# Zero fills moved from GpSimd to the vector engine, the last output projection cut into five full banks, and a new order of the whole program

## The chip, the core and the metric

The kernel runs on one NeuronCore of a Trainium2 chip. Its engines are named here as the profile names them: PE (TensorE, matmuls into PSUM), PEld (its weight loads), DVE (VectorE), ACT (ScalarE), POOL (GpSimd) and SP (SyncE, which in this kernel issues nearly all DMAs). The metric is device microseconds (us) of one execution.

## The reference

Two independent layers over 2048 tokens and 640 features (bf16), whose results stand side by side in one output of 1280 columns.

```python
# A: gated long convolution, columns 0..639
k_shift = sum(k_pad[:, t:t+S] * shift_k[:, 3-t] for t in range(4))
kv = k_shift * v
y = irfft(rfft(kv, 2S) * rfft(ssm_k, 2S))[:S] + kv * ssm_D
a = q * y
# B: segmented attention with a memory, columns 640..1279; 32 heads of 20, N=4 segments of 512
for s in range(4):
    p = softmax(qs @ ks.T * scale + mask)      # mask: -1e9 on keys after the query
    a_dot = p @ vs
    a_mem = (phi(qs) @ M) / (phi(qs) @ z + 1e-6)
    outs.append(g * a_mem + (1 - g) * a_dot)
    M, z = M + phi(ks).T @ vs, z + phi(ks).sum()
b = concat(outs) @ wo
```

## The kernel before

Layer A runs in five blocks of 128 channels (`conv(dp)`). For each block the short filter is a set of matmuls with `kr` (the keys, transposed by the DMA) as weights ("ks"), multiplied by `vt` on DVE. The Fourier transforms are matmuls with the table `Wf`: of the long filter `kT` and of `vt` ("F" groups, eight banks of 512 columns each). DVE does butterflies and the product (`Kh`, `Xh`, `Y`, `pq`), and the inverse is matmuls with `Wi`.

Layer B runs in eight units `u` (`project(u)`, `attend(u)`): segment `u // 2`, half `u % 2` of the heads. `project` makes K, Q and V of four token tiles (five matmuls of 320 columns each, tile `KQ` for K and Q, `Va` for V), turns K and Q into `KQT` (in unit 0 by matmuls with the identity, later by a DMA), and writes a bound of the logits into spare rows of `KQT` by four small DMAs from `bT`. `attend` makes logits in PSUM (weights from `KQT`), exponentials on ACT (`ET`, two of 128x1024 for every set of four heads), and the weighted values by matmuls with `ET` as weights; DVE divides and adds them into `o_s`. `project_out(s)` turns `o_s` and multiplies by `wo`. In the last segment (`last`) the turn is done by matmuls with the identity, one bank for each of five column chunks `cc` of `o_s`, and each bank goes to `xT`.

A row of attention pads and constants is filled once at the start: the unused columns of `KQ`, `PP` (the feature maps phi), `kmx`, the first columns of `kr` and `kb`, and the two memories `Mbd`. `PP[:, 0]` is phi of K and is not written in the last segment; `PP[:, 1]` is phi of Q.

No instruction is issued where it is written: `Recorder.add` (line 151) records every operation, and `issue` (line 245) emits them all from line 257 in the order of a table of numbers (`ORDER`, line 890). `BASE` (line 911) gives each PSUM group its bank, and `EVICT` (line 885) says for each copy out of PSUM whether DVE ("1") or ACT ("0") does it. Each engine then works through its own part of that order, one instruction after the other, and waits at an instruction until what it needs is there. So a late load holds up all that stands behind it on the engine that waits. SP issues DMAs in order too, and the ninth DMA and each later one first waits until the one eight places before it, on the same semaphore, has landed.

The copy that `EVICT` decides is

```python
def evict(self, out, in_, grp):
    ...
    if EVICT[e] == "1":
        self.nc.vector.tensor_copy(out=out, in_=in_, grp=grp)
    else:
        self.nc.scalar.copy(out=out, in_=in_, grp=grp)
```

At the start `WARM` matmuls on a zeroed tile (`o2`, ten of 512 columns) run on PE before there is data.

Of the kernel before, what the change touches and what calls it, by code (L numbers as in the profile page):

```python
# [21 lines left out]
S = 2048; D = 640  # L22
H = 32; DH = 20; NS = 4; L = 512
# [3 lines left out]
KPAD = 16  # L27
# [238 lines left out]
class Layer:  # L266
    def __init__(self, ctx, tc, A_q, A_k, A_v, A_shift_k, A_ssm_k, A_ssm_D, B_x, B_wq, B_wk, B_wv, B_wo, B_beta, out):
# [5 lines left out]
        E = ctx.enter_context  # L273
# [90 lines left out]
        nc.gpsimd.memset(self.PP[:, 1, :, :, DH + 1:DH + 2], 1.0)  # L364
        nc.gpsimd.memset(self.kr[:, 0:KPAD], 0.0)
        self.kb = c.tile([128, KPAD + S], bf16, name="kb")
        nc.gpsimd.memset(self.kb[:, 0:KPAD], 0.0)
# [4 lines left out]
        for h in range(2):  # L372
            nc.gpsimd.memset(self.Mbd[h][0][:], 0.0)
# [459 lines left out]
    def project_out(self, s):  # L833
        nc, rec = self.nc, self.rec
        last = s == NS - 1
        if last:
# [11 lines left out]
            spare = self.PP[:, 0].rearrange("p t h d -> p (t h d)")  # L848
        else:
            oTv = self.ring("xT", None)[:].rearrange("p c q -> p (c q)").rearrange("p (t c q) -> p t c q", t=4, c=5)  # L850
            for t in range(0, 4, 2):
                rec.key = ("oT", s, t)
                nc.sync.dma_start_transpose(out=oTv[:, t:t + 2].rearrange("p t c q -> p (t c) q"), in_=self.o_s[s][:, t:t + 2])
        for t in range(4):
            rec.key = ("W", s, t)
            if last and t < 3:
                outb = spare[:, 640 * t:640 * t + 640].rearrange("p (i j) -> p i j", i=2)
            else:
                outb = self.ring("outb", [128, 2, 320], n=2)[:]
            for i in range(2):  # L860
                if i % WW == 0:
                    g = self.group(WW, "w")
                for part in ((0, 1, 2), (3,), (4,)) if last else ((0, 1, 2, 3, 4),):
                    with rec.one():
                        for cc in part:
                            nc.tensor.matmul(g.ap[:, i % WW, 0:320], lhsT=oTv[:, t, cc, :], rhs=self.wo[:, cc, 320 * i:320 * i + 320], start=(cc == 0), stop=(cc == 4), grp=g)
# [18 lines left out]
EVICT = ("1110001010000101101001001000000000000000000000000000000000010000000000000000000001000100000000100000000000000000000000000000001000000000"  # L885
         "000000000000000100000000001001000000001000100010011000110100000010011010000001101100000010000000000000")
# [100 lines left out]
```

## Time and profile before

| | us |
|---|---|
| median of three runs (lowest, highest) | 273.2 (272.6, 273.31) |
| the profiled execution | 274.12 |
| its span, first to last instruction | 272.3 |
| PE busy | 261.3 (96%) |
| DVE busy | 250.4 (92%) |
| ACT busy | 247.3 (91%) |
| POOL busy | 6.8 (3%) |

The profiled execution is 1.82 us longer than its span, and 0.92 us above the median of the three runs. "Busy" of PE includes matmuls that stand in its pipeline, so 96% doesn't mean PE at its peak. Nearly all instructions have line 257, so they are told apart by tiles: `ET<-ps` is an exponential, `KQ<-ps` a copy of a projection, `F<-ps` one of a transform, and so on. An "x4" in a row of the timeline means four such instructions merged, and the duration then reaches from the first one's start to the last one's end. A bracket says how long the engine had been idle and what ended it.

### The profile page before, as it was taken

The numbers are of one execution on the slowest core, as the hardware profiler recorded it, in microseconds if no ns is written. First come the engines' busy times: TensorE is split into PE (matmuls) and PEld (weight loads), VectorE is DVE, ScalarE is ACT, GpSimd is POOL, SyncE is SP. The second block draws the span as 40 slices with busy tenths as digits, with TensorE's granted clock in tenths as the row PEclk, the third lists the DMA queues.
The fourth block names the chain that finished last, engine by engine and source line by source line (L and its number), as shares of the span: only waits on it lengthen the run. The fifth ranks groups of instructions, "written<-read, shape, count | busy, mean of one in ns | idle before, by whom it ended". The sixth has DMA issues, their size and how long they took to land.

```text
span 272.3 us, 10125 instructions
## 1 busy us (share of the span) xinstructions
PE 261.3 (96%) x4385; PEld 196.4 (72%) x4387; DVE 250.4 (92%) x395; ACT 247.3 (91%) x377; POOL 6.8 (3%) x18
## 2 busy tenths in 40 slices
PE   8789999999999999999999999999999999998994
PEld 3568767868867677776766787768576876766883
DVE  1799999999999999999999999999999999999950
ACT  2356899999999999999999999999999999899954
POOL 8100000000000000000000000000000000000000
PEclk9799999999999999999999999999999999899999
DMA  6999399999959678996896989959964566454233
GB/s 163 293 242 214 70 223 207 211 291 137 182 102 231 214 156 145 177 186 128 167 204 161 224 178 150 178 117 186 197 140 123 59 139 108 85 67 116 75 70 105
DMA packets 126716, 43.73 MB, mean 161 GB/s; under 512 B 117083, under 2 KB 124256, under 8 KB 126544
## 3 DMA queue, kind: packets, MB, share of 16 engines
q1 hardware_dynamic: 126512, 42.91, 79.7%
q8 instruction: 34, 0.56, 0.8%
q0 software_dynamic: 160, 0.19, 0.2%
q14 instruction: 10, 0.08, 0.1%
HBM read 14.11 MB, written 7.34 MB: 79 GB/s over the span
## 4 chain that ended last, share of the span: by engine, by line
PE 60%; ACT 24%; DVE 10%; issue 4%; ACTq 0%; DVEq 0%
PE ps L257 60%; ACT ET L257 15%; ACT F L257 4%; DVE Kh L257 2%; ACT Va L257 2%; DVE F L257 1%; DVE o L257 1%; ACT outb L257 1%; ACT KQ L257 1%; ACT PP L257 1%; DVE pq L257 1%; DVE vt L257 1%; DVE Xh L257 1%; ACT bT L257 1%; DVE qabs L257 0%
## 5 line engine op out<-in xcount | busy, mean ns | idle before, releaser
L257 ACT ACTIVATE ET<-ps 128x1024 bf16<-128x1024 f32 x160 | 165.2, 1140 | 1.0 <-PE ps L257 0.9
L257 PEld LDWEIGHTS <-xT 128*128 128x128 bf16 x640 | 59.0, 98 | 27.2 <-issue 6.4
L257 PE MATMUL ps<-wqkv,xT 128*128 128x320 bf16 x480 | 75.4, 299 | 1.2 <-ACT ET L257 0.6
L257 ACT CAST F<-ps 128x512 bf16<-128x512 f32 x71 | 44.6, 721 | 1.9 <-PE ps L257 1.7
L257 PE MATMUL ps<-Va,ET 128*128 128x21 bf16 x1280 | 41.7, 173 | 0.1
L257 PEld LDWEIGHTS <-ET 128*128 128x128 bf16 x1280 | 39.3, 96 | 2.5 <-issue 1.4
L257 PEld LDWEIGHTS <-Wf 128*128 128x128 bf16 x320 | 29.6, 99 | 7.5 <-DMA Wf<-c_wf 1.3
L257 PE MATMUL ps<-KQT 32*128 32x128 bf16 (+2 forms) x896 | 34.0, 240 | 0.4 <-ACT ET L257 0.3
L257 ACT CAST KQ<-ps 128x320 bf16<-128x320 f32 x52 | 25.3, 537 | 4.2 <-PE ps L257 4.1
L257 PE MATMUL ps<-wo,xT 128*128 128x320 bf16 x160 | 26.4, 304 | 0.6 <-ACT ET L257 0.5
L257 PE MATMUL ps<-kT,Wf 128*128 128x256 bf16 x160 | 23.5, 283 | 1.5 <-DVE kT L257 1.3
L257 PEld LDWEIGHTS <-KQT 32*128 32x128 bf16 x896 | 16.1, 92 | 10.3 <-issue 8.7
L257 PE MATMUL ps<-vt,Wf 128*128 128x256 bf16 x160 | 22.1, 273 | 0.0
L257 PE MATMUL ps<-Y,Wi 128*128 128x256 bf16 x160 | 20.5, 273 | 0.0
L257 PE MATMUL ps<-Mbd,PqT 128*128 128x84 bf16 x96 | 18.2, 203 | 1.0 <-ACT ET L257 0.8
L257 DVE TENSOR_TENSOR Y<-Y,pq 128x2048 bf16<-128x2048 bf16 (+1 forms) x20 | 18.8, 952 | 0.1
L257 DVE TENSOR_TENSOR pq<-Xh,Kh 128x2048 bf16<-128x2048 bf16 x15 | 18.1, 1209 | 0.0
L257 PEld LDWEIGHTS <-Wi 128*128 128x128 bf16 x160 | 14.6, 98 | 3.6 <-issue 1.5
L257 ACT ACTIVATE PP<-KQ 128x1280 bf16<-128x1280 bf16 x12 | 16.7, 1389 | 0.0
L257 PEld LDWEIGHTS <-kr 128*128 128x128 bf16 x116 | 14.7, 149 | 2.2 <-issue 0.4
L257 ACT CAST Va<-ps 128x320 bf16<-128x320 f32 x28 | 14.5, 547 | 0.3 <-PE ps L257 0.2
L257 PE MATMUL ps<-pack 32*128 32x128 bf16 x512 | 14.4, 218 | 0.3 <-ACT ET L257 0.2
(90 smaller groups left out, 373.4 us busy)
## 6 DMA issues: line engine op xcount, KB each, us to landing
vt<-in_A_v_dram SPq DMA_DIRECT2D x10, 256.0 KB
pq<-in_A_q_dram SPq DMA_DIRECT2D x10, 256.0 KB
out_dram<-outb SPq DMA_DIRECT2D x13, 160.0 KB
turned<-kT SPq DMA_DIRECT2D x4, 512.0 KB
kT<-turned SPq DMA_DIRECT2D x4, 512.0 KB
out_dram<-pq SPq DMA_DIRECT2D x8, 256.0 KB
kb<-kr SPq DMA_DIRECT2D x6, 256.0 KB
Wf<-c_wf SPq DMA_DIRECT2D x4, 256.0 KB
```

The source lines that it names most:

```text
L257: f(*[fix(a) for a in args], **{k: fix(v) for k, v in kw.items()})
```

## The change

Three edits.

1. Nine fills of constants (line 360 to 373) go from POOL to DVE; `Drow` stays on POOL. Those of zeros over 2-byte elements are issued over 4-byte elements on DVE, so that their counts are halved (`KQ` 128x1536 becomes 128x768).
2. In the last segment the output projection no longer makes eight groups of 320 columns (four token tiles, two halves). The four tiles of 640 columns are laid side by side, 2560 columns, and cut into five banks of 512. A bank that covers two token tiles takes two matmuls per chunk `cc`, one for each tile's piece, of 128, 256 or 384 columns. All five results go to `PP` (in place of three to `PP[:, 0]` and the fourth to `outb`), and four stores go out from there.
3. `ORDER`, `BASE` and `EVICT` are replaced, and `EVICT` has 235 digits with 32 ones in place of 238 with 36.

```diff
-        nc.gpsimd.memset(self.kmx[:, :, DH:32], 0.0)
-        nc.gpsimd.memset(self.KQ[:, :, :, :, DH:32], 0.0)
-        nc.gpsimd.memset(self.KQ[:, :, 0, :, DH:DH + 1], 1.0)
-        nc.gpsimd.memset(self.PP[:, :, :, :, DH:32], 0.0)
+        nc.vector.memset(self.kmx[:, :, DH:32], 0.0)
+        nc.vector.memset(self.KQ[:, :, :, :, DH:32], 0.0)
+        nc.vector.memset(self.KQ[:, :, 0, :, DH:DH + 1], 1.0)
+        nc.vector.memset(self.PP[:, :, :, :, DH:32], 0.0)
...
         for h in range(2):
-            nc.gpsimd.memset(self.Mbd[h][0][:], 0.0)
+            nc.vector.memset(self.Mbd[h][0][:], 0.0)
...
-            spare = self.PP[:, 0].rearrange("p t h d -> p (t h d)")
...
+        if last:
+            flat = self.PP[:].rearrange("p a t h d -> p (a t h d)")[:, 0:2560]
+            for b in range(5):
+                rec.key = ("W", s, b)
+                g = self.group(1, "w")
+                pieces = [(t, max(0, 512 * b - 640 * t), min(640, 512 * b + 512 - 640 * t)) for t in range(4)]
+                pieces = [p for p in pieces if p[1] < p[2]]
+                for part in ((0, 1, 2), (3,), (4,)):
+                    with rec.one():
+                        for t, lo, hi in pieces:
+                            for cc in part:
+                                nc.tensor.matmul(g.ap[:, 0, 640 * t + lo - 512 * b:640 * t + hi - 512 * b], lhsT=oTv[:, t, cc, :], rhs=self.wo[:, cc, lo:hi],
+                                                 start=(cc == 0 and t == pieces[0][0]), stop=(cc == 4), grp=g, skip_group_check=True)
+                self.evict(flat[:, 512 * b:512 * b + 512], g.ap[:, 0, :], g)
+            for t in range(4):
+                rec.key = ("OB", s, t)
+                self.stores(last).dma_start(out=self.out[L * s + 128 * t:L * s + 128 * t + 128, D:2 * D], in_=flat[:, 640 * t:640 * t + 640])
+            return
         for t in range(4):
...
-            if last and t < 3:
-                outb = spare[:, 640 * t:640 * t + 640].rearrange("p (i j) -> p i j", i=2)
-            else:
-                outb = self.ring("outb", [128, 2, 320], n=2)[:]
+            outb = self.ring("outb", [128, 2, 320], n=2)[:]
...
-EVICT = ("1110001010000101101001001000000000000000000000000000000000010000...
+EVICT = ("0101000110000010100000101000000000000000000000000000000000000000...
```

What the new tables do is seen from the order of the instructions on each engine, before and after. Three places matter below.

First SP at the start, which issues the loads: `Y` receives the first tokens `x`, `kT` the long filter, `kr` the transposed keys, `wqkv` the weights of the projections, `vt` the values of layer A. Before:

```order
L257 DMA ident<-c_ident 128x128
L257 DMA kT_99<-in_A_ssm_k_dram 128x2048
L257 DMA Y_98<-in_B_x_dram 128x640
L257 DMA Wf<-c_wf 128x1024
L257 DMA Y_98<-in_B_x_dram 128x640
L257 DMA Wf<-c_wf 128x1024 x3
L257 DMA Y_98<-in_B_x_dram 128x640 x2
L257 DMA wqkv<-in_B_wk_dram 128x5x320
L257 DMA_TRANSPOSE kr<-in_A_k_dram 128x2048
L257 DMA wqkv<-in_B_wq_dram 128x5x320
L257 DMA vt_103<-in_A_v_dram 128x8x128 x2
```

and with the change:

```order
L257 DMA Y_98<-in_B_x_dram 128x640 x2
L257 DMA ident<-c_ident 128x128
L257 DMA Y_98<-in_B_x_dram 128x640
L257 DMA wqkv<-in_B_wk_dram 128x5x320
L257 DMA Y_98<-in_B_x_dram 128x640
L257 DMA_TRANSPOSE kr<-in_A_k_dram 128x2048
L257 DMA Wf<-c_wf 128x1024
L257 DMA kT_99<-in_A_ssm_k_dram 128x2048
L257 DMA Wf<-c_wf 128x1024
L257 DMA vt_103<-in_A_v_dram 128x8x128
L257 DMA Wf<-c_wf 128x1024 x2
L257 DMA wqkv<-in_B_wq_dram 128x5x320
```

The tokens, the K weights and the transposed keys come first now, the long filter and its Fourier table behind them: PE begins with the K projection, its turns and the short filter, and does the filter's transform after these.

Second DVE at the start (`o_95` is the tile of the warming matmuls, and later of the sigmoid of beta). Before:

```order
L257 MEMSET o_95 128x320
L257 TENSOR_SCALAR o_95<-o_95 128x64
L257 CAST Va_86<-o_95 128x64x2
L257 CAST kT_100<-ps 128x4x128 x2
L257 CAST Va_85<-o_95 128x64x2
L257 CAST taps<-ps 128x40
L257 TENSOR_TENSOR skd_74<-ident,taps 128x512
L257 CAST xT_96<-ps 128x5x128
```

and with the change:

```order
L257 MEMSET PP 128x128x6
L257 MEMSET o_95 128x320
L257 MEMSET kr 128x8
L257 CAST xT_96<-ps 128x5x128
L257 MEMSET KQ 128x128x6
L257 MEMSET Mbd_93 128x176
L257 CAST xT_96<-ps 128x5x128
L257 MEMSET KQ 128x4x16
L257 MEMSET kb 128x8
L257 TENSOR_TENSOR pq_79<-ident,taps 128x512
L257 TENSOR_TENSOR skd_74<-ident,taps 128x512
L257 CAST KQ<-ps 128x16x20 x2
```

The fill of `PP` stands ahead of that of the warming tile, and the sigmoid's TENSOR_SCALAR stands later, behind the copies of K.

Third ACT at the end. Before:

```order
L257 ACTIVATE ET_113<-ps 128x1024
L257 ACTIVATE ET_117<-ps 128x1024 x2
L257 ACTIVATE ET_112<-ps 128x1024 x2
L257 CAST xT_97<-ps 128x512 x2
L257 CAST PP<-ps 128x320 x4
L257 CAST outb_120<-ps 128x320 x2
L257 CAST PP<-ps 128x320 x2
```

and with the change:

```order
L257 ACTIVATE ET_113<-ps 128x1024 x2
L257 ACTIVATE ET_117<-ps 128x1024 x2
L257 ACTIVATE ET_112<-ps 128x1024 x2
L257 CAST xT_97<-ps 128x512 x2
L257 CAST PP<-ps 128x512 x5
```

Eight copies of 320 columns have become five of 512. The copies that ACT does, counted in the two orders, from its first instruction to its first exponential, from there to its last exponential, and behind it:

| copy on ACT | to the first exponential: before, now | between | behind the last |
|---|---|---|---|
| `KQ`, 320 wide | 11, 9 | 41, 46 | 0, 0 |
| `Va`, 320 wide | 3, 2 | 25, 27 | 0, 0 |
| `outb`, 320 wide | 0, 0 | 20, 19 | 2, 0 |
| `F`, 512 wide | 10, 12 | 61, 59 | 0, 0 |
| `KQT`, 512 wide | 8, 7 | 0, 0 | 0, 0 |
| `bT`, 512 wide | 1, 1 | 5, 7 | 0, 0 |
| `xT`, 512 wide | 0, 0 | 3, 2 | 2, 2 |
| `PP`, 320 wide, now 512 | 0, 0 | 0, 0 | 6, 5 |

On DVE there are three `KQ` and one `Va` fewer, one `outb` more; two `bT` fewer, one `KQT` and one `xT` more; and `taps` goes to ACT. PE has 4387 matmuls before and after. Ahead of the first matmul of logits stand 268 of them before and 258 now; the difference is ten matmuls of the projections (75 and 65), and all other kinds have the same count there. POOL issues its four loads in the order `pack`, `skd` (the taps of the short filter), `bt`, `Drow` instead of `bt`, `skd`, `Drow`, `pack`.

More of the change, by code (lines that the diff above doesn't have):

```diff
@@ L862, in project_out @@
                     g = self.group(WW, "w")
[L863 to L866, printed above, removed]
+                with rec.one():
+                    for cc in range(5):
+                        nc.tensor.matmul(g.ap[:, i % WW, 0:320], lhsT=oTv[:, t, cc, :], rhs=self.wo[:, cc, 320 * i:320 * i + 320], start=(cc == 0), stop=(cc == 4), grp=g)
                 if i % WW == WW - 1:
```

54 lines of the change are left out of this document (27 added, 27 removed).

## The prediction

> **What bounds the kernel now.** I read the busy times by stage first, then the chain of waits, then the timelines of the start and the end. I cut the span where ACT starts its first exponential and where it ends its last one.
>
> ```profile
> core 0: us, PE busy (x) PEld busy (x) DVE busy (x) ACT busy (x) POOL busy (x), PEclk, DMA share, GB/s
> 0.00:36.80 36.80, 33.14 (x276) 24.06 (x278) 27.42 (x46) 20.62 (x41) 6.83 (x18) 0.95 0.80 197
> 36.80:261.25 224.45, 220.58 (x4011) 166.65 (x4011) 220.44 (x344) 222.79 (x327) 0.00 (x0) 0.99 0.83 158
> 261.25:272.30 11.05, 7.54 (x102) 5.69 (x98) 2.49 (x6) 3.90 (x10) 0.00 (x0) 0.98 0.34 96
> ```
>
> In the middle ACT is busy 222.79 of 224.45 us, so it is idle for 1.66 us. DVE is idle for 4.01 and PE for 3.87. Three engines are full there at once, and a new order can win next to nothing in it; ACT has the least room. The idle time lies in the first 36.80 us (ACT 16.18, DVE 9.38, PE 3.66) and in the last 11.05 (ACT 7.15). The chain says the same in another way: it runs over all three.
>
> ```profile
> PE 60%; ACT 24%; DVE 10%; issue 4%; ACTq 0%; DVEq 0%
> ```
>
> So I write the span as: start of the first exponential, plus ACT's work from there, plus its 1.66 us of gaps, plus what follows the last exponential. Here are these points, the prices of copies on ACT, and the last store, from the timeline.
>
> ```profile
> 36.80 1.02 ACT L257 ACTIVATE ET<-ps 128x1024 bf16<-128x1024 f32 x1
> 38.94 0.78 ACT L257 CAST KQ<-ps 128x320 bf16<-128x320 f32 x2
> 256.42 4.83 ACT L257 ACTIVATE ET<-ps 128x1024 bf16<-128x1024 f32 x5
> 264.57 1.07 ACT L257 CAST xT<-ps 128x512 bf16<-128x512 f32 x2 [3.32 <-PE ps L257]
> 266.30 1.41 ACT L257 CAST PP<-ps 128x320 bf16<-128x320 f32 x4 [0.65 <-PE ps L257]
> 268.52 0.77 ACT L257 CAST PP<-ps 128x320 bf16<-128x320 f32 x2
> 269.31 0.33 SPq L257 DMA_DIRECT2D out_dram<-PP  x1
> ```
>
> Two copies of 320 columns take 0.78 and four take 1.41, so one more costs (1.41 - 0.78) / 2 = 0.32. Two of 512 take 1.07, 0.53 each.
>
> **ACT's work in the middle.** The two orders' counts: `KQ` +5, `Va` +2, `outb` -1, six more copies of 320 at 0.32: +1.9. `F` -2, `bT` +2, `xT` -1, one fewer of 512 at 0.53: -0.5. Together **+1.4**. Nothing covers it if ACT stays the fullest engine; if ACT had slack, it would cost 0. I take +1.4. DVE gets the reverse: three fewer copies of 320 at 0.483 are -1.4 (one `KQT` and one `xT` more against two `bT` fewer cancel).
>
> ```profile
> L257 DVE CAST KQ<-ps 128x320 bf16<-128x320 f32 x12 | 5.8, 483 | 0.0
> ```
>
> **The fills.** On POOL they cost the span something only through others. On DVE I price them by the one fill that it has already.
>
> ```profile
> 0.88 0.33 DVE L257 MEMSET o<- 128x320 uint32 x1 [0.88 <-PEq L971]
> 5.17 1.40 POOL L257 MEMSET PP<- 128x1536 bf16 x1
> 6.15 1.61 DVE L257 TENSOR_SCALAR o<-o 128x64 f32<-128x64 f32 x1 [4.95 <-ACT o L257]
> 7.80 0.35 DVE L257 CAST Va<-o 128x128 bf16<-128x128 f32 x1
> ```
>
> 320 elements take 0.33, so `KQ` and `PP` with 768 take 0.8 each, the two `Mbd` about 0.2 each, and the five small ones no more than 0.2 each: at most 3.0 in all, and 1 if the size hardly mattered. I take 3.0 and count it as nothing, because DVE has 9.38 us of idle time in that stage; without this cover it is +3.0. `PP`'s fill does delay the warming matmuls by 0.8, but eight of them (at 4.42 / 10 each, row below) then end at 5.6, where ten ended at 5.68.
>
> The TENSOR_SCALAR on 64 elements took 1.61 while POOL was filling; a copy of 128 took 0.35. So up to 1.3 us of the start came from POOL's fills, and it stood ahead of DVE's copies of `kT`, for which PE waited (1.25 us in the row at 9.39 below). The Trainium skill, SBUF — State Buffer, "Who interferes with whom", says that a DVE operation in a 2-port mode and a GpSimd one exclude each other for a whole instruction; the 1.61 agrees. By that rule the 1.3 us go with the fills; by rows alone it stays possible that something else held the TENSOR_SCALAR, and the walk below doesn't use it.
>
> **The start.** PE's rows, two 1 us windows with its clock, and the loads that it waits for:
>
> ```profile
> 1.26 4.42 PE L257 MATMUL ps<-o 128*128 128x512 bf16 x10 [1.26 <-DVE o L257]
> 7.51 0.62 PE L257 MATMUL ps<-ident,skd 5*64 5x5 bf16 x12 [0.29 <-DMA skd<-in_A_shift_k_dram]
> 9.39 1.87 PE L257 MATMUL ps<-kT,Wf 128*128 128x256 bf16 x8 [1.25 <-DVE kT L257]
> 16.59 2.88 PE L257 MATMUL ps<-wqkv,xT 128*128 128x320 bf16 x20
> 19.31 2.82 PE L257 MATMUL ps<-pq,kr 128*128 128x512 bf16 x20
> 25.78 0.61 PE L257 MATMUL ps<-ident,KQ 128*128 128x128 bf16 x8
> 27.98 2.35 PE L257 MATMUL ps<-vt,Wf 128*128 128x256 bf16 x20
> 36.35 0.40 PE L257 MATMUL ps<-KQT 32*128 32x384 bf16 x8
> ```
> ```profile
> 8.00:9.00 1.00, 0.14 (x4) 0.05 (x2) 1.00 (x3) 0.00 (x0) 0.00 (x0) 0.96 1.06 398
> 9.00:10.00 1.00, 0.61 (x4) 0.45 (x5) 0.96 (x4) 0.00 (x0) 0.00 (x0) 0.50 1.04 383
> ```
> ```profile
> 1.95 0.52 POOL L257 DMA_DIRECT2D skd<-in_A_shift_k_dram  x1
> 2.10 0.43 SPq L257 DMA_DIRECT2D Wf<-c_wf  x1
> 2.57 0.43 SPq L257 DMA_DIRECT2D Y<-in_B_x_dram  x1
> 8.55 4.71 SPq L257 DMA_TRANSPOSE kr<-in_A_k_dram  x1
> SPq L257 <- DMA Wf<-c_wf: 1.8, 1, 1.8
> ```
>
> The prices from these rows: a projection matmul 2.88 / 20 = 0.144, short filter 0.141, a turn 0.61 / 8 = 0.076, a transform 2.35 / 20 = 0.118. The K weights are now the fifth load, issued where the fifth was (2.57). The first `Wf`, the fourth load, was waited for by SP until 8.55, 6.45 after its issue, with 704 KB ahead of it; `wk` has 512 KB ahead and is larger (400 for 256 KB), so I let it land 6.45 after its issue too, at 9.0. The taps come earlier: `skd` landed 7.51 - 1.95 = 5.56 after its issue, and standing second on POOL it is issued near 1.3, so its matmuls run at 6.9.
>
> From 9.0 PE has, up to the first logits: 65 projections 9.4, 28 of the short filter 3.9, 32 turns of K and Q and 16 of the filter 3.6, 5 to 10 turns of x 0.6, 66 transforms 7.8, eight small ones 0.6. The sum is 25.9, so 34.9 with no wait. The same prices give 21.5 for before's stretch from 16.59 (75 projections 10.8, short filter 3.9, 32 turns 2.4, 32 transforms 3.8, small 0.6), which took 36.35 - 16.59 = 19.76, since a row's end includes the pipeline. Scaled by 19.76 / 21.5 the 25.9 become 23.8, and the logits start at 32.8. That is 3.5 earlier than 36.35 if nothing waits, and 1.4 earlier if the waits and a slow clock at the start eat 2.1. I take **-2.5** for the first exponential, and as bounds -3.5 and +1.5 (the first rival).
>
> **The end.** PE's and DVE's rows behind the last exponential:
>
> ```profile
> 262.70 1.38 PE L257 MATMUL ps<-wo,xT 128*128 128x320 bf16 x9
> 263.35 0.89 DVE L257 TENSOR_TENSOR o_s<-ps,rr 128x320 bf16<-128x320 f32 x2
> 263.93 1.06 PE L257 MATMUL ps<-ident,o_s 128*128 128x128 bf16 x16
> 264.82 3.97 PE L257 MATMUL ps<-wo,xT 128*128 128x320 bf16 x28
> ```
>
> Before, both last chunks are turned behind the last `o_s` (264.24), and 28 matmuls of 320 follow: 3.97 / 8960 columns = 0.44 ns a column. Now the fourth chunk is turned earlier, only eight turns follow `o_s` (0.53, until 264.9), and its copy (0.53) runs beside 2048 columns that don't need it. 6144 columns remain from 265.5, 2.7 us, until 268.2, and one copy of 512 until 268.8, where the last copy ended at 268.52 + 0.77 = 269.29. That is **-0.4**; 0 if the wide last bank eats it. The store behind it has 160 KB as before.
>
> **The sum:** -2.5 + 1.4 - 0.4 = -1.5. Against the profiled execution: span 272.3 to 270.8, time 274.12 to 272.6. The median of the runs is 0.92 below that execution, so 273.2 - 1.5 = **271.7**. A measurement of this kernel tells from no change what is over 0.3%, below 272.4 or above 274.0.
>
> **The rivals.** (1) *Slower: the transposed load blocks SP.* `kr` took SP 4.71 us to issue and now stands ahead of `Wf`, the long filter and `vt`. Issued from about 3.6 it frees SP at 8.3; `vt`, the fourth behind it, goes out at 9.7 and by the 6.45 above lands at 16.2. The short filter's banks can't be emptied without `vt`; PE wants to begin there at 13.5. If PE stands for it and for the filter behind it, 2.7 us and more, then the 2.5 are gone, and with up to 1.5 us of delay the sum is +1.4 - 0.4 + (0 to 1.5): 274.2 to 275.7. It decides from a first exponential later than 35.8. For it speaks that 4.71; against it that the walk reaches the short filter's last bank only at 17.4, so that the first banks alone wait. Chance 0.22.
>
> (2) *The same: the clock.* PE's clock was 0.50 after a second with 0.14 busy. The new start has short pieces of work between waits up to 9.0. If the clock is at half for 3.4 us of the K projection, PE loses 1.7: 271.7 + 1.7 = 273.4. The Trainium skill, TensorE: Matmul & The Clock Gate, "What's actually happening", has the full clock only after some 3.4 us of sustained work; the windows above agree with a drop after idling, and by this rule eight warming matmuls (3.5 us) hardly suffice. Chance 0.13.
>
> (3) *The same: gaps on ACT in the middle.* 1.66 us of gaps in 224.45 is little to keep with another order. With 1 to 2 us more: 272.7 to 273.7. Here too belongs that the five banks bring nothing (+0.4). Chance 0.15.
>
> (4) *Much faster: DVE is what binds.* With 4.01 us of gaps it it is less likely than ACT with 1.66, but the chain gives DVE 10% too. Then the +1.4 on ACT is free and DVE's -1.4 counts: 273.2 - 2.5 - 1.4 - 0.4 = 268.9. Chance 0.10.
>
> **How the numbers follow.** The forecast has 0.40, with its own range of 270.6 to 272.9 (the start between -3.5 and -1.4, the end between -0.5 and 0). The range of 8 in 10 reaches down to near rival 4 and up through most of rival 1: 269.0 to 275.0. Faster by over 0.3%: 0.32 from the forecast, 0.10 from (4), 0.05 from (2) and (3) and 0.02 from (1), 0.49. Slower: most of (1), 0.17, and tails of (2) and (3), 0.08: 0.25. Within 0.3%: 0.26.
>
> **What would show it.** Right: the first exponential between 33 and 35.5; ACT busy about 1.4 more in the stretch between first and last exponential, with gaps near 1.7; 10.5 to 10.8 from the last exponential to the end; no POOL fill and a TENSOR_SCALAR near 0.35. Wrong: a first exponential later than 35.8 with PE waiting for `vt`, `kT` or `Wf`; gaps on ACT of 3 us or more in the middle; or a middle that is shorter although ACT has more to do, which would say that ACT wasn't the bound.

## The result, and the profile after

The changed kernel takes 270.79 us (median of five runs, 270.28 to 271.58) where the kernel before took 272.60 beside it (272.17 to 273.31). The ratio is 0.9929, with a 95% interval of 0.9903 to 0.9955: faster by 0.7%. In a second series, beside three of the experiments, it was 271.48 against 273.04, 0.9938 (0.9908 to 0.9968). The forecast was 271.7. Three executions far slower than all others, one of the kernel before at 346.11 and two of a kernel below (20 matmuls more) at 289.54 and 587.99, stand in no comparison.

The profiled execution of the changed kernel took 271.58 us, with a span of 269.8; the one of the kernel before took 274.12, with a span of 272.3. The windows by stage of the changed kernel, cut at the first and the last exponential as the prediction cut them (length; then busy time and instructions of PE, weight loads, DVE, ACT and POOL; then the granted clock, DMA share and GB/s):

```profile
0.00:32.73 32.73, 30.32 (x267) 22.34 (x268) 24.98 (x49) 19.71 (x40) 2.57 (x9) 1.00 0.79 196
32.73:258.86 226.13, 221.19 (x4026) 166.69 (x4025) 222.26 (x347) 224.16 (x332) 0.00 (x0) 1.00 0.85 159
258.86:269.80 10.94, 7.27 (x97) 5.12 (x95) 2.37 (x6) 3.81 (x7) 0.00 (x0) 1.00 0.38 115
```

Against before, the first exponential comes 4.07 us earlier (36.80 to 32.73). The middle is 1.68 longer: ACT has 1.37 more to do (222.79 to 224.16) and 0.31 more of gaps (1.66 to 1.97). The end is 0.11 shorter. Together that is -2.50: the start gains, and the middle gives part of it back. The granted clock reads 1.00 in all three rows, where before had 0.95, 0.99 and 0.98; this turns out to be a good part of the answer.

The start of the changed kernel, PE's timeline (start, length, operation, count):

```profile
6.79 0.62 PE L257 MATMUL ps<-ident,skd 5*64 5x5 bf16 x12
8.07 0.84 PE L257 MATMUL ps<-wqkv,xT 128*128 128x320 bf16 x5
12.88 2.83 PE L257 MATMUL ps<-pq,kr 128*128 128x512 bf16 x21
28.78 3.57 PE L257 MATMUL ps<-wqkv,xT 128*128 128x320 bf16 x25
32.28 0.40 PE L257 MATMUL ps<-KQT 32*128 32x384 bf16 x8
```

PE begins its projections at 8.07, and the first logits come 24.2 us later. The transposed load of `kr` holds SP from 3.65 on, yet the short filter that reads it runs from 12.88 with no wait in its row. On DVE the fills show, and the small TENSOR_SCALAR that had taken 1.61:

```profile
0.97 0.70 DVE L257 MEMSET PP<- 128x768 uint32 x1 [0.97 <-PEq L984]
7.30 0.70 DVE L257 MEMSET KQ<- 128x768 uint32 x1
13.46 0.18 DVE L257 TENSOR_SCALAR o<-o 128x64 f32<-128x64 f32 x1
```

The end, ACT's timeline and then PE's last row:

```profile
262.69 0.58 ACT L257 CAST xT<-ps 128x512 bf16<-128x512 f32 x1 [1.17 <-PE ps L257]
263.78 2.05 ACT L257 CAST PP<-ps 128x512 bf16<-128x512 f32 x4 [0.50 <-PE ps L257]
266.17 0.58 ACT L257 CAST PP<-ps 128x512 bf16<-128x512 f32 x1 [0.34 <-PE ps L257]
```
```profile
262.49 3.64 PE L257 MATMUL ps<-wo,xT 128*128 128x384 bf16 x25
```

The last copy ends at 266.75, 7.89 us behind the last exponential; before it was 8.04 (269.29 - 261.25). The five banks brought a tenth of a microsecond or two.

### The profile page after: what moved, and what is told of

Same layout as the page of the kernel before. It is cut to its first block, busy times and chain, and to the rows that moved or that the text cites. A ratio compares the mean times of both kernels' runs of the same rounds, so it can differ in the third digit from the quotient of the medians.

```text
span 269.8 us, 10110 instructions
## 1 busy us (share of the span) xinstructions
PE 258.8 (96%) x4387; PEld 194.2 (72%) x4387; DVE 249.6 (93%) x400; ACT 247.7 (92%) x378; POOL 2.6 (1%) x9
## 4 chain that ended last, share of the span: by engine, by line
PE 55%; ACT 35%; DMA 4%; issue 3%; DVE 1%; SPq 0%; ACTq 0%; DVEq 0%
PE ps L257 55%; ACT ET L257 23%; ACT F L257 5%; ACT PP L257 2%; ACT Va L257 2%; ACT KQ L257 2%; DMA out_dram<-outb 2%; DMA KQT<-KQ 1%; DMA pq<-in_A_q_dram 1%; ACT outb L257 1%; ACT xT L257 1%; ACT bT L257 0%; DVE xT L257 0%; DVE o_s L257 0%; DVE PP L257 0%
## 5 line engine op out<-in xcount | busy, mean ns | idle before, releaser
L257 PEld LDWEIGHTS <-xT 128*128 128x128 bf16 x640 | 58.1, 98 | 26.5 <-issue 4.8
L257 ACT CAST F<-ps 128x512 bf16<-128x512 f32 x71 | 41.9, 682 | 2.0 <-PE ps L257 2.0
L257 PE MATMUL ps<-Va,ET 128*128 128x21 bf16 x1280 | 40.1, 172 | 0.1
L257 PEld LDWEIGHTS <-ET 128*128 128x128 bf16 x1280 | 38.1, 96 | 1.9 <-issue 1.2
L257 PE MATMUL ps<-wo,xT 128*128 128x320 bf16 (+4 forms) x160 | 25.7, 299 | 0.8 <-ACT ET L257 0.8
L257 PE MATMUL ps<-kT,Wf 128*128 128x256 bf16 x160 | 21.8, 273 | 0.0
L257 PE MATMUL ps<-pack 32*128 32x128 bf16 x512 | 13.8, 215 | 1.1 <-ACT ET L257 0.9
```

Of the source, the lines that this page charges most:

```text
L257: f(*[fix(a) for a in args], **{k: fix(v) for k, v in kw.items()})
```

## What the clock does in the kernel before

The record of each run has its mean granted clock. The 87 runs of the kernel before that stood beside the experiments fall into three groups by it:

| mean clock | runs | medians in three series, us | median spans, us |
|---|---|---|---|
| 0.997 to 1.000 | 22 | 272.1 to 272.5 | 270.4 to 270.7 |
| 0.992 to 0.994 | 30 | 273.1 to 273.2 | 271.3 to 271.5 |
| 0.986 to 0.987 | 35 | 274.3 to 274.4 | 272.5 to 272.6 |

A step is 0.7 to 1.4 us in the three series, about 1.0 in the mean. The execution that the prediction argued from, at 0.986, is of the third group. It shows two places with the clock at half: one from 9.0 to 12.4, of which the prediction quoted the first microsecond, and a second one in the middle. Windows of 1 us of the kernel before (the clock stands third from the end):

```profile
228.00:229.00 1.00, 0.48 (x18) 0.50 (x16) 1.00 (x3) 1.00 (x2) 0.00 (x0) 1.00 0.53 182
...
231.00:232.00 1.00, 1.00 (x42) 0.97 (x43) 0.92 (x3) 1.00 (x2) 0.00 (x0) 0.50 0.29 64
232.00:233.00 1.00, 1.00 (x34) 0.69 (x27) 1.00 (x3) 0.47 (x2) 0.00 (x0) 0.50 1.00 204
233.00:234.00 1.00, 1.00 (x5) 0.60 (x4) 1.00 (x3) 1.00 (x2) 0.00 (x0) 0.50 1.09 220
```

Both stand some 2 us or less behind a microsecond in which PE had little to do (0.14 at 8, 0.48 at 228), and both last near 3.4 us. Such a microsecond is not enough, though: the same profile has one at 0.48 from 249 to 250 with no drop behind it, and in the profile of a kernel below (the late load of `kr`) PE stands idle for 2.06 us and the clock keeps 1.00. Nor is it needed: another (the new start with the old rest) falls to half at 230, and no microsecond of the ten ahead of that has PE below 0.73. All 17 runs of the changed kernel have 0.997 or more.

So the difference of the medians in the second series parts in two: 273.04 - 272.14 = 0.9 us is the clock (272.14 is the median of before's 14 runs at full clock there), and 272.14 - 271.48 = 0.7 us is everything else. In the first series the clocks of before's five runs are not known. Three of them, 272.17, 272.54 and 272.60, lie where the other series have runs at full clock (272.11 to 272.77), so that the remainder there is between 272.17 - 270.79 = 1.4 and 272.60 - 270.79 = 1.8.

## The experiments

Two readings stood against each other at first: the new order of the start makes the gain and the fills are nothing (A, the prediction's), or POOL's fills hold up DVE and through it PE (B). A third (C in the first group) was that the order behind the start matters as much. "C" in the last group is the clock.

### The fills back on POOL, in the changed kernel

```diff
-        nc.vector.memset(self.PP[:, :, :, :, DH:32], 0.0)
+        nc.gpsimd.memset(self.PP[:, :, :, :, DH:32], 0.0)
 (and so the other eight fills)
```

> The changed kernel with its nine fills back on POOL; nothing else is altered. Theory A (the fills bring nothing, the order of the start does): first exponential within 0.4 us of the changed kernel's 32.73, time within 0.5 us of its 270.8. Rival B (POOL's fills hold up DVE, and DVE's work holds up PE): the TENSOR_SCALAR on 64 elements takes about 1.6 us again where it took 0.18, the first exponential starts 0.8 to 1.3 us later, at 33.5 to 34.0, and the time goes to 271.6 to 272.1.

It took 271.48 us, 0.9942 (0.9915 to 0.9969), the same as the changed kernel's 271.48 in the second series. Its windows and one row of POOL's timeline:

```profile
0.00:32.87 32.87, 30.22 (x267) 22.21 (x268) 22.91 (x40) 19.73 (x41) 6.41 (x18) 1.00 0.76 195
32.87:258.28 225.41, 220.89 (x4026) 166.58 (x4025) 221.99 (x347) 223.94 (x332) 0.00 (x0) 1.00 0.84 160
```
```profile
2.76 0.53 POOL L257 DMA_DIRECT2D skd<-in_A_shift_k_dram  x1
3.45 1.41 POOL L257 MEMSET KQ<- 128x1536 bf16 x1
```

The first exponential is at 32.87, where the changed kernel has 32.73, and 32.87 in a second profile. The TENSOR_SCALAR took 0.18, since it now runs at 13.60 and POOL's last fill ends at 6.95. In the new order A holds for the start and the median. Two things are left. POOL issues the load of `skd` behind the fill of `PP`, at 2.76 and not at 1.92, and PE waits 0.78 us for it and is busy for 0.22 of the microsecond from 6 to 7. And two of the seven runs, at 272.80 and 272.93, have a clock of 0.994 and 0.993, where none of the changed kernel's 17 is below 0.997. Whether the fills cost clock here too is not shown by so few.

### The fills on DVE alone, in the kernel before

```diff
-        nc.gpsimd.memset(self.PP[:, :, :, :, DH:32], 0.0)
+        nc.vector.memset(self.PP[:, :, :, :, DH:32], 0.0)
 (and so the other eight fills)
```

> The kernel before with its nine fills on DVE; nothing else is altered. Theory A: first exponential within 0.4 us of 36.80, time within 0.5 us of 272.6. Rival B: the TENSOR_SCALAR falls from 1.61 us to about 0.2, the first exponential comes 0.8 to 1.3 us earlier, at 35.5 to 36.0, and the time falls to 271.3 to 271.8.

It took 272.35 us, 0.9962 (0.9942 to 0.9983), 1.0 less than the kernel before beside it (273.35). Rows of DVE, of PE and the first two stages:

```profile
6.19 0.20 DVE L257 TENSOR_SCALAR o<-o 128x64 f32<-128x64 f32 x1 [4.99 <-ACT o L257]
6.56 0.72 DVE L257 CAST kT<-ps 128x512 bf16<-128x512 f32 x1
```
```profile
8.51 1.03 PE L257 MATMUL ps<-kT,Wf 128*128 128x256 bf16 x8 [0.32 <-DVE kT L257]
```
```profile
0.00:35.80 35.80, 32.56 (x277) 23.63 (x278) 28.10 (x53) 20.66 (x41) 2.61 (x9) 1.00 0.79 203
35.80:259.36 223.56, 219.70 (x4012) 166.15 (x4011) 220.28 (x346) 222.65 (x327) 0.00 (x0) 1.00 0.83 158
```

In the old order B holds, by every number of the start that it gave: 0.20 where 1.61 stood, PE's wait for `kT` 0.32 and not 1.25, the eight transforms in 1.03 and not 1.87, the first exponential at 35.80. The time that B gave, 271.3 to 271.8, did not come. Ten of its twelve runs have a clock of 0.998 or more, and lie between 272.0 and 272.65, where the kernel before lies at full clock too. So either the freed DVE or the clock is what brings the 1.0; the run with warming further down tells them apart.

The Trainium skill, SBUF — State Buffer, "Who interferes with whom", has DVE, in its 2-port modes, and GpSimd exclude each other at their shared port. The trace agrees: the same instruction takes 1.61 while POOL fills, and 0.20 and 0.18 in the two kernels where POOL doesn't.

### The start of the one order with the rest of the other

Both are edits of the table that sets the order, and of the engines of the copies that belong to it. The first has the changed kernel's list up to the first logits and then what is left of before's list in its sequence; the second the reverse.

```diff
 ORDER = 
-  before[0:187] + before[187:]
+  after[0:177]  + (before without after[0:177])
```

> Up to the first logits the changed kernel's order, with its fills on DVE; from there the order, the engines of the copies and the last projection of the kernel before. Theory A (ACT is full from the first exponential on, so that the whole gain is made at the start, and the new rest gives 1.6 us of it back): first exponential at 32.7 +- 0.4, ACT's work between first and last exponential 222.5, time 272.6 - 4.1 - 0.3 = 268.3 (267.8 to 269.0). Rival C (three engines are full in the middle, and an order made for a later start doesn't use the earlier one): first exponential at 32.7 all the same, ACT's gaps in the middle 3 us or more in place of 1.66, time 270.0 or more.

> Up to the first logits the order of the kernel before, with its fills on POOL; from there the changed kernel's order, its engines for the copies and its last projection in five banks. Theory A: first exponential at 36.8 +- 0.4, ACT's work in the middle +0.1 against the kernel before (two more copies of 320, one fewer of 512), gaps about 2.0, end 10.9: time 272.6 + 0.1 + 0.3 - 0.1 = 272.9 (272.3 to 273.6). Rival C: the new rest is what gains, at 271.5 or less.

The new start with the old rest took 272.37 us, 0.9955 (0.9936 to 0.9974); the old start with the new rest 274.89, 1.0059 (1.0034 to 1.0084). The first two stages of the one, and PE's projections ahead of its first logits:

```profile
0.00:34.67 34.67, 32.32 (x287) 23.84 (x288) 27.49 (x53) 21.06 (x43) 2.57 (x9) 1.00 0.83 203
34.67:260.13 225.46, 220.58 (x4002) 166.10 (x4001) 221.02 (x345) 222.73 (x326) 0.00 (x0) 0.99 0.82 158
```
```profile
28.01 6.28 PE L257 MATMUL ps<-wqkv,xT 128*128 128x320 bf16 x45
```

And of the other:

```profile
0.00:38.16 38.16, 34.56 (x286) 25.04 (x287) 26.60 (x44) 21.47 (x43) 6.84 (x18) 0.96 0.82 200
```

A is wrong in both. It expected 268.3 and 272.9. In the new start, the 45 projections where the changed kernel has 25 say why the first exponential came at 34.67: what is left of the old list has 20 projections of the next piece ahead of its first logits, which the expectation did not count. They are not lost, only done earlier. ACT then has 2.73 us of gaps in the middle (225.46 - 222.73), but 0.97 of them lie from 230 to 234, where this execution's clock is at half. So C, which expected 32.7 and gaps of 3 us or more, isn't shown either. At full clock this kernel has a median of 272.2 in ten runs, and the kernel before has 272.5 in four of the same series: the new start alone gains next to nothing.

The profile of the old start is that of the slowest of its nine runs, 277.02 with a mean clock of 0.988. Seven others have 0.998 or more, with a median of 274.7, 2.2 above the kernel before at full clock. There are ten matmuls more ahead of the first exponential (286 against 276), which comes 1.36 later than in the profile of before (36.80), both with the clock at half from 9 on, and the middle is 1.66 longer (226.11 against 224.45). The start and the rest of an order can't be priced apart; only the pair that was made together keeps the gain.

### The last projection in eight groups again

```diff
-            for b in range(5):
-                g = self.group(1, "w")
+        for t in range(4):
+            for i in range(2):
+                g = self.group(WW, "w")
```

> The changed kernel with the last output projection in eight groups of 320 columns and its result in the ring tiles, as before; everything up to the last exponential is as in the changed kernel. Theory A (the end is 0.1 us of the gain): last exponential where the changed kernel has it, 11.0 to 11.1 us from there to the end where it has 10.94, time within 0.4 us of the changed kernel. Rival E (the wide banks are what the end gains by, as the prediction had it): the end takes 11.3 to 11.5 us, time 0.4 to 0.6 us longer.

> The changed kernel itself, beside the next three, as their measure. Every theory: 270.8 us within 0.5, first exponential at 32.7, gaps on ACT in the middle near 2.0.

It took 271.57 us, 0.9941 (0.9915 to 0.9967), against the changed kernel's 271.48. Its last stage:

```profile
258.33:269.50 11.17, 7.48 (x99) 5.53 (x96) 2.37 (x6) 4.00 (x10) 0.00 (x0) 1.00 0.37 113
```

The changed kernel, profiled once more on the same chip, has 10.92 there:

```profile
32.87:258.38 225.51, 220.97 (x4026) 166.60 (x4025) 222.14 (x347) 224.04 (x332) 0.00 (x0) 1.00 0.86 160
258.38:269.30 10.92, 7.27 (x97) 5.12 (x95) 2.37 (x6) 3.81 (x7) 0.00 (x0) 1.00 0.38 116
```

So the banks are worth 0.25 us in the profile, half of what E expected and too little for the times to tell.

### Six copies to DVE, six copies to ACT, a fifth of a projection less for PE

The three ask which engine sets the middle of the changed kernel. In the first, five copies of `KQ` and one of `outb`, all of 320 columns, go from ACT to DVE; in the second, five and one others go from DVE to ACT. The third leaves out one of the five chunks `cc` in the output projection of the first three segments.

```diff
 EVICT (digits of six copies in the middle)
-0 0 0 0 0 0      (ACT)
+1 1 1 1 1 1      (DVE);  the second kernel the reverse, on six others
```
```diff
-                    for cc in range(5):
+                    for cc in (0, 1, 2, 4):
```

> The changed kernel with six of its 320-column copies between the first and the last exponential moved from ACT to DVE; order and banks stay. ACT's work falls by 6 x 0.32 = 1.9 us, DVE's grows by 6 x 0.483 = 2.9, and DVE had 3.9 us without work there. Theory A (ACT sets the length of the middle): first to last exponential 1.9 us shorter, time 268.9 +- 0.5. Rival F (DVE is as full as ACT): the middle grows by 1.0 to 2.9, time 271.8 to 273.7. Rival P (PE's work sets it; PE's span less its busy time was 11.0, 11.0, 10.6 and 10.8 us in four kernels): within 0.5 us of 270.8.

> The changed kernel with six 320-column copies between first and last exponential moved the other way, from DVE to ACT: ACT's work +1.9 us, DVE's -2.9. Theory A (ACT alone sets the middle, although the six moved to DVE cost 4.0 us): the middle 1.9 us longer, time 272.7 to 273.9. Rival F (DVE sets it): the middle 1.0 to 2.9 shorter, 268.0 to 270.0. Rival H (order and engines are balanced against each other, every shift costs): 1.0 to 4 us longer, with more gaps on ACT than the 1.5 to 2.0 of the changed kernel, and not only more work.

> The changed kernel without one of the five contraction chunks of the output projection of the first three sequences, so that their output is incomplete: 24 matmuls of 320 columns fewer in the middle, PE's work 24 x 0.144 = 3.5 us less; ACT, DVE and all loads and stores as before. Theory A: the middle stays within 0.5 us, time 270.3 to 271.3. Rival P: the middle falls by 2 to 3.5 us, time 267.3 to 268.8.

Six to DVE: 275.29 us, 1.0068 (1.0043 to 1.0093). Six to ACT: 273.22, 0.9999 (0.9973 to 1.0025). Without the fifth: 270.76, 0.992 (0.9891 to 0.995). Their middles, in this order:

```profile
32.12:261.64 229.52, 222.65 (x4026) 166.97 (x4025) 224.03 (x353) 223.85 (x326) 0.00 (x0) 0.99 0.83 157
```
```profile
32.44:260.20 227.76, 221.80 (x4026) 167.03 (x4025) 220.29 (x341) 226.19 (x338) 0.00 (x0) 1.00 0.83 158
```
```profile
34.34:259.86 225.52, 219.46 (x4002) 165.06 (x4001) 222.12 (x347) 224.03 (x332) 0.00 (x0) 1.00 0.84 160
```

- PE is not what sets it: with 24 matmuls less and 1.5 us less of busy time the middle is 225.52, where the changed kernel has 225.51. P, which asked for 2 to 3.5 us, falls. The medians differ by 0.7 (270.76 against 271.48), with intervals that overlap, so a small share of PE isn't excluded.
- More work on ACT costs in full: ACT is busy 2.15 us more, the middle is 2.25 longer, and the gaps are what they were (1.57 and 1.47). This is A's answer, and not H's, which asked for more gaps.
- Less work on ACT brings nothing if DVE has to take it. ACT's busy time fell by 0.19 only, its gaps grew from 1.47 to 5.67, and the middle is 4.0 longer, beyond even F's 2.9. Part of that is one stretch at half clock in this profile (its mean is 0.992); the three runs of this kernel at a mean clock of 1.00 give the loss as about 3 us (274.46 to 274.77 against 271.48). This is F's answer, at its upper end. DVE now has 11% of the chain of waits, where the changed kernel (second row) has 1%:

```profile
PE 52%; ACT 31%; DVE 11%; issue 5%; ACTq 0%; DVEq 0%
PE 52%; ACT 38%; issue 4%; DMA 3%; DVE 1%; ACTq 0%; DVEq 0%
```

A busy time of ACT is thus no fixed sum of work. The exponentials of the changed kernel and of this one (with six copies on DVE; busy time, mean ns of one, idle time before):

```profile
L257 ACT ACTIVATE ET<-ps 128x1024 bf16<-128x1024 f32 x160 | 163.4, 1116 | 1.1 <-PE ps L257 1.1
```
```profile
L257 ACT ACTIVATE ET<-ps 128x1024 bf16<-128x1024 f32 x160 | 160.7, 1086 | 4.0 <-PE ps L257 3.8
```

The mean of one is longer where ACT has fewer gaps, because the records of neighbours overlap: behind the last exponential of the changed kernel four copies of 512 take 2.05 and one alone 0.58, so that each further one adds 0.49. A gap lets one record stand alone. ACT has 21 gaps of more than 0.02 us in this middle and 7 in the changed kernel's; as an estimate from these rows, 14 gaps more at 0.09 give back 1.3 of the 1.7 us by which the busy time fell short of -1.9. The idle time ahead of the exponentials ends at PE's results, 3.8 of 4.0 us, so the six copies on DVE reach ACT through PE.

### The transposed load of kr behind Wf, kT and vt

```diff
 SP's queue
-  DMA_TRANSPOSE kr
   Wf, kT, Wf, vt
+  DMA_TRANSPOSE kr
```

> The changed kernel with the transposed load of kr, which holds SP for 4.3 us from 3.65 on, moved behind Wf, kT and the first vt on SP. Theory A (its early place is right, because the short filter needs it at 12.9): kr is issued near 5 and frees SP near 9.5, its data come 1 to 3 us after the filter could begin; first exponential 0.5 to 2.5 us later, time 271.5 to 273.5. Rival 1 of the prediction, in its weak form (early kr delays Wf, kT and vt, and PE would gain by the other order): first exponential earlier than 32.3, time below 270.8.

It took 273.70 us, 1.0008 (0.9985 to 1.0032): the whole gain is gone. Part of that is the clock, at 0.991 to 0.994 in five of its twelve runs; the median of the seven others is 273.28, 1.8 above the changed kernel. PE's row and SP's:

```profile
14.90 2.87 PE L257 MATMUL ps<-pq,kr 128*128 128x512 bf16 x21 [2.06 <-DMA kr<-in_A_k_dram]
```
```profile
5.80 7.06 SPq L257 DMA_TRANSPOSE kr<-in_A_k_dram  x1
```

PE stands for `kr` for 2.06 us, and the first exponential comes at 34.79 and not at 32.87. This is A. Where that load stands is worth 2 us, and its early place is the right one: it must lie ahead of the reads, and what stands behind it in the queue (`vt` at 9.52) is needed only later.

### More to do for PE at the start

In the kernel before, 20 matmuls on the identity behind those of the taps; in the changed kernel the fill for the warming first on DVE and three more warming matmuls.

```diff
                 nc.tensor.matmul(tp[:, 4 + t, :], lhsT=skr..., rhs=self.ident[0:5, 0:5], ...)
+            for _ in range(20):
+                nc.tensor.matmul(g.ap[:, 0, 128:256], lhsT=self.ident[:], rhs=self.ident[:], start=True, stop=True, grp=g)
```
```diff
                 with rec.one():
+                  for _ in range({7: 4}.get(n, 1)):
                     nc.tensor.matmul(g.ap[:, 0, 0:WARMC], lhsT=idle[:, 0:128], ...)
```

> The kernel before with 20 more matmuls of 128 columns on the identity behind those of the taps, into unused columns of their bank: about 1.4 us of work for PE where it was busy for 0.14 of the us from 8 to 9, just ahead of the stretch at clock 0.50. Nothing else is altered. Theory C (that gap lets the clock fall, and the slow clock is why the first exponential comes at 36.8): clock 1.00 from 8 to 13 us, the 20 projections start at 14.6 to 15.2 and not at 16.59, the first exponential at 34.9 to 35.9, mean clock 0.998 or more in nearly all runs, median 272.2 (271.8 to 272.6). Rival G (PE waits for DVE and the loads there, and the slow clock costs nothing): first exponential at 36.8 or, by the added work, up to 0.5 later, median 273.0 to 273.6.

> The changed kernel with the fill for the warming matmuls first on DVE, so that they start at about 1.2 us and not at 2.07, and three more of them, so that they still reach to the first turns of x at 5.6. Theory C (in some runs, as in the one without a fifth of the output projection, PE runs the first projections at half its rate, 2.76 us for ten and not 1.80, because warming began late): the first exponential at 32.0 to 32.8, no run above 272.2, median 270.6 to 271.3. Rival: no change, median 271.1 to 271.7 with single runs above 273.

The kernel before, kept at work, took 272.23 us, 0.9952 (0.9929 to 0.9976); eight of the ten runs compared lie between 272.12 and 272.39, at 0.997 or more. PE's and DVE's rows, and the windows at the start and by stage:

```profile
7.90 1.29 PE L257 MATMUL ps<-ident 128*128 128x128 bf16 x20
9.41 1.03 PE L257 MATMUL ps<-kT,Wf 128*128 128x256 bf16 x8 [0.22 <-DVE kT L257]
15.52 2.88 PE L257 MATMUL ps<-wqkv,xT 128*128 128x320 bf16 x20
```
```profile
6.20 1.59 DVE L257 TENSOR_SCALAR o<-o 128x64 f32<-128x64 f32 x1 [5.00 <-ACT o L257]
```
```profile
9.00:10.00 1.00, 0.78 (x10) 0.58 (x8) 0.96 (x4) 0.00 (x0) 0.00 (x0) 1.00 1.05 388
```
```profile
0.00:35.73 35.73, 33.13 (x297) 24.49 (x298) 27.30 (x46) 20.62 (x42) 6.86 (x18) 1.00 0.81 203
35.73:259.53 223.80, 219.70 (x4012) 166.12 (x4011) 220.29 (x344) 222.74 (x327) 0.00 (x0) 1.00 0.83 158
```

This tells the two apart. The TENSOR_SCALAR still takes 1.59, and the transforms start at 9.41, as late as before (9.39); only the clock is 1.00, so that they take 1.03 and not 1.87. The first exponential comes at 35.73, as with the fills on DVE (35.80), 1.07 earlier than in the profile of before. Work that computes nothing made the kernel faster, and DVE's 1.4 us alone did not matter. With the fills on DVE the microsecond from 8 to 9 has PE busy for 0.68 and not for 0.14, so the fills helped the old order in the same way, through the clock. G falls. The 20 projections start at 15.52, later than the 14.6 to 15.2 that C gave. Not explained is the second stretch of before's profile: eight of the ten runs have neither, although a microsecond at 0.49 is still there, at 227.

The Trainium skill, TensorE: Matmul & The Clock Gate, "What's actually happening", describes an activity window of 3.4 us that runs on its own and is not set by the kernel's start. With that it would be chance whether a gap as short as these falls on a window that counts as idle, and one drop would last about 3.4 us. The length of the stretches at 0.50 agrees, and so does it that only some executions of one kernel have them; the window itself no run here shows.

The changed kernel with more warming took 270.96 us, 0.9900 (0.9866 to 0.9934), none of its six runs above 271.50. The changed kernel has two of twelve above 273 in its second series, on another chip. PE waits for the identity's load instead, and the first exponential is at 32.62:

```profile
6.01 0.72 PE L257 MATMUL ps<-ident,Y 128*128 128x128 bf16 x10 [0.43 <-DMA ident<-c_ident]
```

The intervals overlap, so it is not shown to be faster than the changed kernel; the median of the changed kernel's first series, 270.79, is as low.

## Why the prediction was right, and where it was wrong

The time was right (271.7 against 270.79 and 271.48), but three of its terms were mis-sized, and what it called a risk of the change was a cost of the kernel before. At full clock the profiled spans differ by 1.3 (270.6 of the warmed kernel before, 269.3 of the changed one), where the forecast had -1.5. That the two are so near is in part luck: the start gained 0.36 more than forecast, while the gaps cost 0.41 and the end brought 0.25 less. And the sum had nothing for the clock of the kernel before, which is part of what the medians show.

- **The start, -2.5.** It was -4.07 against the profile of before. The walk itself held: it had PE's projections at 9.0 and the logits 23.8 us later; they were at 8.07 and 24.2 later. What failed is the deduction behind it, 1.0 us for waits and a slow clock: in PE's rows there is one wait of 0.24, and the granted clock is 1.00. With the projections 0.9 earlier than assumed, -4.07 lies even beyond its bound of -3.5. And 1.07 of the 4.07 is the half clock from 9.0 to 12.4 in before's own profile. Against before at full clock (35.73) the start gains 2.86. About half of that is work which only changed sides of the cut: PE is busy 30.46 us ahead of the first exponential and 220.97 in the middle, where the kernel before with warming has 33.13 - 1.29 = 31.84 and 219.70. The start of one execution is known to about 1 us only: in five profiles of kernels with this same start, the changed one among them twice, the first exponential lies between 31.90 and 32.87. The one at 31.90 (the last projection in eight groups) has its last exponential at 258.33, where the changed kernel has 258.38: its earlier start won nothing.
- **ACT's work in the middle, +1.4.** Measured +1.37, and +1.30 against the warmed kernel (222.74 to 224.04). The six copies to ACT show that such work is paid in full. This step was right.
- **ACT's gaps, 0.** They grew by 0.31, and by 0.41 against the warmed kernel (1.06 to 1.47). Rival 3's mechanism, at a third of its price.
- **The end, -0.4.** It was -0.11 and -0.15. The forecast had the last copy 7.55 us behind the last exponential, which against 8.04 is -0.5 and not the -0.4 that it wrote; it ends after 7.89. The copy of the last turns was done at 4.41 and not at 4.25, the matmuls behind it end at 7.27 (262.49 + 3.64 - 258.86) and not at 6.95, and the wide copy takes 0.58 and not 0.53. Against eight groups in the same order the banks bring 0.25.
- **The fills, 0.** Right for the new order, but for its clock, which stays open. In the old one they bring 1.0, by the clock, which the prediction did not see: it had both rows, the 1.61 and the 0.14 busy with 0.50 behind it, and took them for two things.
- **Rival 1**, SP blocked by `kr`: the mechanism is real and worth 2 us, but the change stands on the good side of it. PE did not wait for `vt` or the filter.
- **Rival 2**, the clock: priced as a loss of the change; it was a loss of the kernel before, in 65 of its 87 runs, once or twice, at about 1.0 us each. In its proper form it makes 0.9 of the 1.6 us gained in the second series, and at most 0.4 of the 1.8 in the first.
- **Rival 4**, DVE binds: wrong as a forecast, since ACT's +1.4 was not free. But DVE is close: it can't take six copies more.

What stays open: which part of the new order yields the 0.7 to 1.8 us that remain at full clock. The end gives 0.15 of it, the early place of `kr` is needed for it, and the two halves of the order could not be tested apart. Open too is what makes the clock fall behind one thin microsecond and not behind another.

## What to carry to other kernels

Look at the granted clock of the profiled execution before a sum is made against it: a stretch at 0.50 in the profile of before is time that a change may win by chance, and that another execution of the same kernel doesn't lose. Where PE has a thin microsecond near the start, a few matmuls that compute nothing are the cheapest test of it (here 1.29 us of them won 1.07). And a span cut at an event shows work that moved across the cut as a gain on one side; count the busy time on both sides before believing it.

## What the runs showed of the hardware that was not expected

- The clock fell to 0.50 not only at the start but also at 231 us, deep in a middle in which PE is busy 98% of the time, some 2 us behind one microsecond at 0.48. Each such stretch cost about 1.0 us of the whole. Yet in the profile with the late load of `kr` PE stood idle for 2.06 us and the clock stayed at 1.00.
- Matmuls can run at half their rate while the granted clock reads 1.00. In the profiled execution without the fifth of the projection, ten projections took 2.76 us, where the changed kernel has ten in 1.80 (10.12), with 0.267 us from one start to the next in place of 0.136, and the first exponential came 1.5 us later:

```profile
8.85 2.76 PE L257 MATMUL ps<-wqkv,xT 128*128 128x320 bf16 x10
```
```profile
9.00:10.00 1.00, 1.00 (x6) 0.48 (x4) 0.91 (x2) 0.00 (x0) 0.00 (x0) 1.00 0.94 209
```

  That execution had its time at 272.54, and the other nine lie between 270.41 and 271.13. Whether the two runs of the changed kernel above 273 had the same, no profile shows.
- The transposed load held SP for 4.26 us when issued at 3.65, for 4.71 at 8.55 in the kernel before, and for 7.06 at 5.80, behind four more loads than in the first case. That the loads under way make the difference is likely, but no run varies them alone.
